# Windowed attention and a feed-forward layer in one kernel: two triangles of visible keys merged into one square, transposed once and selected apart on POOL

## The chip, the cores and the metric

One NeuronCore of a Trainium2 chip runs one program. The metric is the device time of that program in microseconds (us), the median over runs. The engines are named as in the profile: PE (TensorE), DVE (VectorE), ACT (ScalarE), POOL (GpSimd) and SP (SyncE, which here only issues transfers).

## The reference, cut to what matters

```python
# q, k, v: (B=8, H=8, S=576, D=64); w_in: (512, 2048); w_out: (2048, 512)
scores = scale * np.matmul(q, k.transpose(0, 1, 3, 2))
rel = pos[:, None] - pos[None, :]
mask = (rel >= 0) & (rel < 128)                      # each query sees itself and the 127 keys before it
scores = np.where(mask, scores + slopes[h] * -abs(rel), -1e9)
attn = exp(scores - max(scores)); attn = attn / (sum(attn) + 1e-9)
x = np.matmul(attn, v)                               # (B, H, S, D) -> 4608 tokens of 512
h = x @ w_in
out = (h / (1 + exp(-1.702 * h))) @ w_out
```

A query at position p sees the keys p-127 to p. For a block of 128 queries these lie in two blocks of 128 keys: in the block of the same positions it sees those at or below its own place (one triangle), in the block before it those above its own place (the other triangle). In columns taken modulo 128 each row therefore sees every column exactly once, and the two triangles fit together into one full square.

## The kernel before

**Feed-forward.** The 4608 tokens are taken in 18 chunks of 256. For each of 16 slices `f` of the inner width, `up(f)` makes `h_ps` with 12 products, ACT, DVE and ACT make `g` and its upper part `gh`, POOL makes its lower part `gl = g - gh`, and `down(f)` adds six products into two accumulators: `gh` by both halves of `w2` (four), then `gl` (two). Everything of 32 bits is split so into an upper and a lower part, since PE multiplies the type `fp32r`. `up(f+1)` is written ahead of `down(f)`.

**Attention** runs beside it, ahead of the chunks that need it. The first two batches (`WholeUnit`, 24 units) are multiplied in plain float32 while the weights are still being decoded. The other six batches are 24 head pairs; the change concerns these. A pair's two heads of 576 positions stand one behind the other as 1152 rows, nine blocks of 128 (`pair_blocks`); a `Unit` is two blocks, the last unit of a pair one, so a pair has five units. Block 4 holds the end of one head and the start of the next; `live` is the first column with keys of the right head (128 in block 0, which has no block before it; 64 in block 5).

A unit passes through stages, one per tick; `tick()` lets five units stand in five stages at once:

- loads of `rq`, `rk` and `rv` (SP's queue, in the order of the program), then the splits `Q`, `K1`/`K2`, `VV` on ACT, DVE and POOL
- `scores`: two products a block into `s_ps`, 128 queries by 256 keys
- `biased` (DVE): adds the mask and slope table `bias`, negates, writes `pb` and the row's minimum `mins`
- `exponents` (ACT): exponential of `pb` with its row sum; `normal` (DVE): scaling with the reciprocal `rec`
- `flip` (PE): transposes each 128x128 part of `pb` that has a key, into `t_ps`
- `high` (ACT) and `low` (DVE): the upper part `ph` and the lower part `pl` of the transposed weights
- `mix` (PE, one tick later): for each chunk of 128 keys two products into `x_ps`: all queries that see these keys (the own block and the next one, 256 columns) by the upper, then by the lower part
- `sum_up`: the sum of upper and lower rows goes to the chunk's `x`, by way of `xb` (the `carry` between two segments on POOL)

A pair has 17 of the 128x128 parts: two a block, and one in block 0.

**Order.** The program is written tick by tick: after each slice `f`, a pace worked out from the chunk that needs a batch next says whether one or more ticks follow. A scheduler then sets the order on each engine; SP's transfers, and the first eight decodings, keep the program's order. Each engine works its queue in order. Buffers rotate in pools: `rq`, `rk` three each, `pb` five, `ph` and `pl` two each.

Of the kernel before, what the change touches and what calls it, by code (L numbers as in the profile page):

```python
# [8 lines left out]
F32 = mybir.dt.float32  # L9
F32R = mybir.dt.float32r  # L10
# [10 lines left out]
P = 128  # L21
# [120 lines left out]
def tile_kernel(ctx: ExitStack, tc: tile.TileContext, q0, k0, v0, qT, kT, v, w_in, w_out, out):  # L142
# [25 lines left out]
    def tables():  # L168
# [65 lines left out]
    def load(u):  # L234
# [7 lines left out]
        u.rq = raw.tile([P, 2 * P], F32, name="rq", tag="rq")  # L242
# [4 lines left out]
    def load_whole(u):  # L247
# [5 lines left out]
        else:  # L253
            u.rq = raw.tile([P, 2 * P], F32, name="rq", tag="rq")
# [84 lines left out]
    def biased(u):  # L339
        u.mins = att.tile([P, 4], F32, name="mins", bufs=3)  # L340
        if u.whole:
            u.p = []
            for i, (at, rows) in enumerate(u.blocks):
                cs = slice(max(u.k0 - at + P, 0), P + rows)
                for hh in range(2):
                    if hh:
                        p = att.tile([P, 3 * P], F32, name="pb", tag=("K1", "K2")[i])
                    else:
                        p = att.tile([P, 2 * P], F32, name="pb", bufs=5)
# [7 lines left out]
        for e, b in enumerate(u.blocks):  # L357
            b.p = att.tile([P, 2 * P], F32, name="pb", bufs=5)
# [7 lines left out]
            if b.live > b.first:  # L366
                nc.gpsimd.memset(b.p[:, :b.live], 0.0)

    def exponents(u):
# [9 lines left out]
        for e, b in enumerate(u.blocks):  # L379
            live = b.p[:b.rows, b.live:b.end]  # L380
# [5 lines left out]
    def normal(u):  # L386
# [17 lines left out]
        for e, b in enumerate(u.blocks):  # L404
            live = b.p[:rows, b.live:b.end]
            nc.vector.tensor_scalar(live, live, u.rec[:rows, e:e + 1], None, ALU.mult)  # L406

    def flip_whole(u):
        u.pt = []
        for hh in range(2):  # L410
            t = ps.tile([P, 4 * P], F32, name="t_ps", bufs=2)
            pt = att.tile([P, 4 * P], F32, name="pw", tag=("ph", "pl")[hh])
# [16 lines left out]
    def flip(u):  # L429
# [5 lines left out]
        u.ph = att.tile([P, 4 * P], F32R, name="ph")  # L435
        u.pl = att.tile([P, 4 * P], F32R, name="pl")
        u.pspans = []
        w = 0
        for c in u.chunks:
            start = w  # L440
            for b, col in c.parts:
                nc.tensor.transpose(  # L442
                    u.t[:c.n, w:w + b.rows], b.p[:b.rows, col:col + c.n], ident[:b.rows, :b.rows])
                w += b.rows
            c.p = u.ph[:c.n, start:w], u.pl[:c.n, start:w]
            if u.pspans and u.pspans[-1][0] == c.n:
                u.pspans[-1][2] = w
            else:
                u.pspans.append([c.n, start, w])

    def high(u):
        if u.whole:
            return
        for m, a, z in u.pspans:
            nc.scalar.copy(u.ph[:m, a:z], u.t[:m, a:z])  # L455
# [318 lines left out]
```

## Time and profile before

| | |
|---|---|
| median of 3 runs | 1079.72 us (1078.15 to 1080.79) |
| profiled execution | 1078.13 us, of which 1076.2 us from first to last instruction |
| granted PE clock | 0.994 of full |
| PE busy | 1054.8 us, 98% |
| DVE, POOL, ACT busy | 706.1, 598.3, 585.7 us |

Busy time is the time in which at least one instruction of the engine runs. Products on PE overlap each other, so a product's duration is longer than the time by which it moves the next one; that time is read from rows of several products. In the groups "x408" is the number of instructions; the numbers behind the bar are the busy time, the mean duration in ns, and the idle time of the engine ahead of them with what ended it. In a stage's row the engines stand in the order PE, PEld (loading of the stationary operand), DVE, ACT, POOL, then the clock and the transfers.

### The profile page before, as it was taken

What the parts mean: (1) busy time and instruction counts of PE and PEld (TensorE: products, weight loads), DVE (VectorE), ACT (ScalarE), POOL (GpSimd) and SP (SyncE); (2) the same over time, 40 slices, a digit from 0 to 9 for tenths busy, and PEclk for the clock granted to TensorE, in tenths of its full rate; (3) what the DMA queues carried; (4) which work ended last, traced back from release to release, by engine and by line L of the source; (5) the groups of instructions that cost most, each with busy time, mean ns of one, the idle gap of its engine ahead of it and who ended that gap; (6) DMA issues with size and microseconds to landing.
All of it is one profiled execution on the core that took longest, in us unless ns stands there. A gap on an engine that the chain in (4) does not pass through costs nothing.

```text
span 1076.2 us, 21415 instructions
## 1 busy us (share of the span) xinstructions
PE 1054.8 (98%) x7041; PEld 930.7 (86%) x7041; DVE 706.1 (66%) x2195; ACT 585.7 (54%) x1773; POOL 598.3 (56%) x855
## 2 busy tenths in 40 slices
PE   8788999999999999999999999999999999999998
PEld 5566777789998999999999999999899999998987
DVE  7999953378898787645667668767868687413131
ACT  5867754366666566444555566656665556332222
POOL 3666842367676676554555657656666566323232
PEclk9989999999999999999999999999999999999999
DMA  8862101233222232111222123222222221000000
GB/s 307 294 234 59 33 13 41 67 87 88 79 81 83 63 89 66 58 27 59 65 64 66 57 64 86 65 73 66 86 66 85 56 59 46 3 18 20 1 21 19
DMA packets 88110, 78.45 MB, mean 73 GB/s; under 512 B 36800, under 2 KB 79296, under 8 KB 88000
## 3 DMA queue, kind: packets, MB, share of 16 engines
q1 hardware_dynamic: 82240, 67.14, 21.4%
q10 hardware_dynamic: 5760, 9.96, 2.5%
q8 instruction: 55, 0.90, 0.3%
q14 instruction: 55, 0.45, 0.1%
HBM read 67.63 MB, written 9.44 MB: 72 GB/s over the span
## 4 chain that ended last, share of the span: by engine, by line
PE 88%; DVE 9%; ACT 1%; issue 1%; DMA 1%; POOL 0%; SPq 0%; DVEq 0%; ACTq 0%; POOLq 0%
PE h_ps L552 35%; PE acc L571 35%; PE s_ps L334 5%; PE x_ps L499 5%; PE t_ps L442 4%; DVE wc L213 2%; DVE wc L212 2%; DVE rw L211 1%; PE x_ps L476 1%; DVE pb L351 1%; PE t_ps L419 1%; PE s_ps L324 1%; PE sb_ps L324 1%; DVE rec L392 1%; DMA rw<-w_out 1%
## 5 line engine op out<-in xcount | busy, mean ns | idle before, releaser
L562 POOL TENSOR_TENSOR gl<-g,gh 128x256 fp32r<-128x256 f32 x288 | 219.6, 763 | 295.0 <-ACT gh L561 237.2
L552 PE MATMUL h_ps<-xh,w 128*128 128x256 f32 x2304 | 373.9, 285 | 2.9 <-DVE g L558 1.8
L552 PEld LDWEIGHTS h_ps<-xh,w 128*128 128x128 f32 x2304 | 330.7, 189 | 38.2 <-DVE g L558 3.3
L571 PE MATMUL acc<-w,gh 128*128 128x512 f32 x1152 | 326.1, 400 | 1.5 <-ACT gh L561 1.4
L558 DVE SCALAR_TENSOR_TENSOR g<-g,h_ps 128x256 f32<-128x256 f32 x288 | 119.3, 415 | 192.2 <-ACT g L557 190.8
L557 ACT ACTIVATE g<-h_ps 128x256 f32<-128x256 f32 x288 | 109.7, 381 | 229.3 <-PE h_ps L552 202.1
L571 PEld LDWEIGHTS acc<-w,gh 128*128 128x128 f32 x1152 | 196.5, 189 | 30.2 <-ACT gh L561 2.4
L552 PE MATMUL h_ps<-xl,w 128*128 128x256 f32 x1152 | 194.8, 281 | 0.0
L561 ACT CAST gh<-g 128x256 fp32r<-128x256 f32 x288 | 116.6, 405 | 133.9 <-DVE g L558 125.2
L571 PE MATMUL acc<-w,gl 128*128 128x512 f32 x576 | 188.6, 402 | 0.5 <-POOL gl L562 0.5
L552 PEld LDWEIGHTS h_ps<-xl,w 128*128 128x128 f32 x1152 | 164.0, 189 | 6.0 <-POOL w L217 0.4
L312 POOL TENSOR_TENSOR K<-rk,K 128x384 fp32r<-128x384 f32 (+1 forms) x120 | 108.9, 907 | 73.8 <-ACT Q L292 15.4
L381 ACT ACTIVATE pb<-pb,mins 128x256 f32<-128x256 f32 (+2 forms) x216 | 104.9, 487 | 46.5 <-DVE mins L362 45.1
L571 PEld LDWEIGHTS acc<-w,gl 128*128 128x128 f32 x576 | 92.7, 189 | 9.1 <-POOL gl L562 0.7
L406 DVE TENSOR_SCALAR pb<-pb,rec 128x256 f32<-128x256 f32 (+2 forms) x216 | 95.2, 477 | 3.3
L311 POOL TENSOR_TENSOR Q<-rq,Q 64x256 fp32r<-64x256 f32 (+1 forms) x120 | 82.6, 688 | 19.7 <-DVE g L558 4.3
L392 DVE TENSOR_SCALAR rec<-sums 128x2 f32<-128x2 f32 (+3 forms) x144 | 49.8, 346 | 59.6 <-ACT pb L381 53.3
L362 DVE CUSTOM_DVE_ANT_0 pb<-s_ps,bias 128x256 f32<-128x256 f32 (+3 forms) x240 | 85.5, 377 | 4.9 <-PE s_ps L334 3.6
L334 PE MATMUL s_ps<-K,Q 128*128 128x256 f32 (+1 forms) x432 | 79.6, 289 | 0.5 <-DVE mins L362 0.5
L461 DVE TENSOR_TENSOR pl<-t_ps,ph 128x512 fp32r<-128x512 f32 (+2 forms) x120 | 72.1, 603 | 6.2 <-ACT ph L455 3.5
L442 PE MATMUL t_ps<-ident,pb 128*128 128x128 f32 x408 | 74.9, 272 | 0.0
L310 DVE CAST K<-rk 128x384 fp32r<-128x384 f32 (+1 forms) x120 | 50.9, 424 | 31.0 <-PE s_ps L334 29.4
(68 smaller groups left out, 1345.9 us busy)
## 6 DMA issues: line engine op xcount, KB each, us to landing
rk<-kT SPq DMA_DIRECT2D x72, 192.0 KB, 2.5
rq<-qT SPq DMA_DIRECT2D x96, 128.0 KB, 2.3
out<-o ACTq DMA_DIRECT2D x36, 256.0 KB, 2.1
rw<-w_in SPq DMA_DIRECT2D x16, 512.0 KB, 5.6
rw<-w_out SPq DMA_DIRECT2D x16, 512.0 KB, 6.5
rk<-kT SPq DMA_DIRECT2D x48, 128.0 KB, 2.2
rv<-v SPq DMA_DIRECT2D x96, 64.0 KB, 1.9
rq<-q SPq DMA_DIRECT2D x16, 128.0 KB, 2.4
```

Of the source, the lines that this page charges most:

```text
L312: nc.gpsimd.tensor_tensor(K2, rk, K1.bitcast(F32), ALU.subtract)
L334: nc.tensor.matmul(u.s[:b.rows, e, b.first:b.end], u.Q[:, b.q0 - u.q0:b.q0 - u.q0 + b.rows], k[:, ko:ko + b.end - b.first], start=(z == 0) ...
L362: nc.vector.tensor_tensor_reduce(b.p[ra:rb, cs:b.end], u.s[ra:rb, e, cs:b.end], bias[head][ra:rb, cs:b.end], -SCALE, BIG, ALU.add, ALU.min ...
L381: nc.scalar.activation(live, live, AF.Exp, bias=u.mins[:b.rows, e:e + 1], scale=-1.0, accum_out=u.sums[:b.rows, e:e + 1],)
L406: nc.vector.tensor_scalar(live, live, u.rec[:rows, e:e + 1], None, ALU.mult)
L442: nc.tensor.transpose(u.t[:c.n, w:w + b.rows], b.p[:b.rows, col:col + c.n], ident[:b.rows, :b.rows])
L552: nc.tensor.matmul(h, w1[f][:, z, k * P:(k + 1) * P], x[:, k], start=(n == 0), stop=(n == len(ops) - 1))
L557: nc.scalar.activation(g, h, AF.Tanh, scale=0.851)
L558: nc.vector.scalar_tensor_tensor(g, g, 1.0, h, ALU.add, ALU.mult)
L561: nc.scalar.copy(gh, g)
L562: nc.gpsimd.tensor_tensor(gl, g, gh.bitcast(F32), ALU.subtract)
L571: nc.tensor.matmul(acc, g[:, t * P:(t + 1) * P], w2[f][:, z], start=(f == self.f0 and n == 0), stop=(f == self.f1 - 1 and n == 2))
```

## The change

The two triangles of a block are merged before the exponential, and the merged square is transposed, split and then taken apart:

- `biased` still writes `pb` with 256 columns and takes the minimum. Columns without keys are set to a large value (`FAR`): in block 0 this is a new memset of 128x128 on POOL; in block 5 an existing memset changes its value and its place. Then DVE takes the minimum of the two halves, column by column, into the first half: in each column one of the two is masked.
- `exponents` and `normal` work on 128 columns of a block instead of up to 256.
- `flip` makes one transpose a block: 9 a pair instead of 17. `high` and `low` work on 128 columns a block, into one buffer `ph` that holds both parts.
- New in `low`: POOL selects the triangles apart. `affine_select` keeps the part on one side of the diagonal and writes zero on the other, for the upper and lower part in one instruction (128 rows by 2 x 128). One select writes the block's own half of its chunk's tile `pc`, one the second half of the chunk before: 17 a pair.
- `mix` has the same products, reading `pc`.
- To make room, `rq` has two buffers instead of three, `pb` four instead of five, `ph` one; the tiles of `flip_whole` share the four `pc` buffers, and the third unit's `rq` uses a buffer of `Q`.

```diff
+        for i, block in enumerate(blocks):
+            block.own, block.before = chunks[i], chunks[i - 1] if i else None
...
         for e, b in enumerate(u.blocks):
-            b.p = att.tile([P, 2 * P], F32, name="pb", bufs=5)
+            b.p = att.tile([P, 2 * P], F32, name="pb", bufs=4)
+            if b.live:
+                nc.gpsimd.memset(b.p[:, :b.live], FAR)
...
-            if b.live > b.first:
-                nc.gpsimd.memset(b.p[:, :b.live], 0.0)
+
+            b.p = b.p[:, :P], b.p[:, P:]
+            nc.vector.tensor_tensor(b.p[0], b.p[0], b.p[1], ALU.min)
+            b.p = b.p[0]
...
-        u.ph = att.tile([P, 4 * P], F32R, name="ph")
-        u.pl = att.tile([P, 4 * P], F32R, name="pl")
...
-            for b, col in c.parts:
-                nc.tensor.transpose(
-                    u.t[:c.n, w:w + b.rows], b.p[:b.rows, col:col + c.n], ident[:b.rows, :b.rows])
...
+        u.pt = att.tile([P, 2, 2 * P], F32R, name="ph", bufs=1)
+        for e, b in enumerate(u.blocks):
+            nc.tensor.transpose(u.t[:, e * P:(e + 1) * P], b.p, ident)
...
+        n = len(u.blocks) * P
+        nc.vector.tensor_tensor(u.pt[:, 1, :n], u.t[:, :n], u.pt[:, 0, :n].bitcast(F32), ALU.subtract)
+        for e, b in enumerate(u.blocks):
+            part = u.pt[:, :, e * P:(e + 1) * P]
+            b.own.p = att.tile([P, 2, 2 * P], F32R, name="pc", bufs=4)
+
+            nc.gpsimd.affine_select(
+                out=b.own.p[:, :, :P], in_=part, pattern=[[0, 2], [1, P]], base=0, channel_multiplier=-1,
+                compare_op=ALU.is_ge, fill=0.0)
+            if b.before:
+                nc.gpsimd.affine_select(
+                    out=b.before.p[:, :, P:], in_=part, pattern=[[0, 2], [-1, P]], base=-1, channel_multiplier=1,
+                    compare_op=ALU.is_ge, fill=0.0)
...
-                    g.x[:, a:a + c.width], c.v, c.p[z],
+                    g.x[:, a:a + c.width], c.v, c.p[:, z, :c.width],
```

The scheduler places the instructions anew. The place shown is the hand-over between two token chunks early in the blockwise attention: the last slice of one chunk (weights `w_15`) has been multiplied, and the first `gl` of the next chunk (weights `w_0`, `w_1`) is due. The names are those of the stages above; `xl` is the lower part of a chunk's `x`. On POOL, before:

```order
L538 TENSOR_TENSOR xl<-xf,xh 128x256 x2
L300 TENSOR_TENSOR VV<-rv,VV 128x2x64
L523 TENSOR_TENSOR xb<-xb,carry 64x128
L300 TENSOR_TENSOR VV<-rv,VV 128x2x64
L562 TENSOR_TENSOR gl<-g,gh 128x256
L367 MEMSET pb 128x64
L311 TENSOR_TENSOR Q<-rq,Q 64x128
L312 TENSOR_TENSOR K_4620<-rk,K_4619 128x256
L562 TENSOR_TENSOR gl<-g,gh 128x256 x2
```

On POOL now, the last twelve rows ahead of the next chunk's first two `gl`:

```order
L465 AFFINE_SELECT pc<-ph 128x2x128
L305 TENSOR_TENSOR VV<-rv,VV 128x2x64
L529 TENSOR_TENSOR xb<-xb,carry 64x128
L317 TENSOR_TENSOR K_4905<-rk,K_4904 128x384
L305 TENSOR_TENSOR VV<-rv,VV 128x2x64
L316 TENSOR_TENSOR Q<-rq,Q 64x256
L461 AFFINE_SELECT pc<-ph 128x2x128
L465 AFFINE_SELECT pc<-ph 128x2x128
L461 AFFINE_SELECT pc<-ph 128x2x128
L465 AFFINE_SELECT pc<-ph 128x2x128
L365 MEMSET pb 128x128
L568 TENSOR_TENSOR gl<-g,gh 128x256 x2
```

Before, three POOL instructions of attention stood between two `gl` here; now 35 stand between the `gl` of `w_15` and that of `w_0`, 17 of them selects (the first 24 are not shown).

On PE, before, from the products of attention at that place to the first that reads the new chunk's `gl`:

```order
L499 MATMUL x_ps<-ph,VV 128x256
L499 MATMUL x_ps<-pl,VV 128x256
L442 MATMUL t_ps<-ident,pb 128x128 x4
L552 MATMUL h_ps<-xh,w_2_578 128x256 x8
L552 MATMUL h_ps<-xl,w_2_578 128x256 x4
L499 MATMUL x_ps<-ph,VV 128x256
L552 MATMUL h_ps<-xh,w_3_598 128x256 x4
L571 MATMUL acc_4589<-w_0_457,gh 128x512 x2
L571 MATMUL acc_4589<-w_0_457,gl 128x512
```

On PE now:

```order
L558 MATMUL h_ps<-xh,w_3_598 128x256 x7
L577 MATMUL acc_4690<-w_0_457,gh 128x512
L577 MATMUL acc_4691<-w_0_457,gh 128x512
L577 MATMUL acc_4690<-w_0_457,gh 128x512
L577 MATMUL acc_4691<-w_0_457,gh 128x512
L505 MATMUL x_ps<-pc,VV 128x256 x2
L558 MATMUL h_ps<-xh,w_3_598 128x256
L558 MATMUL h_ps<-xl,w_3_598 128x256 x4
L339 MATMUL s_ps<-K_4904,Q 128x256
L577 MATMUL acc_4690<-w_0_457,gl 128x512
L577 MATMUL acc_4691<-w_0_457,gl 128x512
```

The products that read `gl` have moved behind other work: ahead of the first of them now stand all of `up(3)` and a product of scores. From the last product by the `gl` of `w_15` to the first by the `gl` of `w_0`, PE has 42 products of `h_ps`, 18 of `x_ps`, 11 of `s_ps`, 8 transposes and 4 of the accumulators.

More of the change, by code (lines that the diff above doesn't have):

```diff
@@ L171, in tables @@
         make_identity(nc, ident)
-        rel_i = raw.tile([P, 2 * P], I32, name="rel_i", tag="rq")
+        rel_i = raw.tile([P, 2 * P], I32, name="rel_i", tag="rq", bufs=2)
         nc.gpsimd.iota(rel_i, pattern=[[-1, 2 * P]], base=P, channel_multiplier=1)
-        rel = raw.tile([P, 2 * P], F32, name="rel", tag="rq")
+        rel = raw.tile([P, 2 * P], F32, name="rel", tag="rq", bufs=2)
         nc.vector.tensor_scalar(rel, rel_i, -1.0 / SCALE, None, ALU.mult)
@@ L241, in load @@
         u.nk = u.q0 + u.nq - u.k0
-        u.rq = raw.tile([P, 2 * P], F32, name="rq", tag="rq")
+        u.rq = raw.tile([P, 2 * P], F32, name="rq", tag="rq", bufs=2)
         u.rk = raw.tile([P, 3 * P], F32, name="rk", tag="rk")
@@ L253, in load_whole @@
         else:
-            u.rq = raw.tile([P, 2 * P], F32, name="rq", tag="rq")
+            if u.at == DEPTH - 1:
+                u.rq = att.tile([P, 2 * P], F32, name="rq", tag="Q")
+            else:
+                u.rq = raw.tile([P, 2 * P], F32, name="rq", tag="rq", bufs=2)
             u.rk = raw.tile([P, 3 * P], F32, name="rk", tag="rk")
@@ L348, in biased @@
                     else:
-                        p = att.tile([P, 2 * P], F32, name="pb", bufs=5)
+                        p = att.tile([P, 2 * P], F32, name="pb", bufs=4)
                     e = 2 * i + hh
@@ L379, in exponents @@
         for e, b in enumerate(u.blocks):
-            live = b.p[:b.rows, b.live:b.end]
+            live = b.p
             nc.scalar.activation(
@@ L404, in normal @@
         for e, b in enumerate(u.blocks):
-            live = b.p[:rows, b.live:b.end]
-            nc.vector.tensor_scalar(live, live, u.rec[:rows, e:e + 1], None, ALU.mult)
+            nc.vector.tensor_scalar(b.p, b.p, u.rec[:rows, e:e + 1], None, ALU.mult)
     def flip_whole(u):
@@ L411, in flip_whole @@
             t = ps.tile([P, 4 * P], F32, name="t_ps", bufs=2)
[L412 removed]
+            pt = att.tile([P, 4 * P], F32, name="pw", tag="pc", bufs=4)
             u.pt.append([])
@@ L434, in flip @@
         u.t = ps.tile([P, 4 * P], F32, name="t_ps", bufs=2)
-        u.ph = att.tile([P, 4 * P], F32R, name="ph")
-        u.pl = att.tile([P, 4 * P], F32R, name="pl")
[L437 to L440, printed above, removed]
-            for b, col in c.parts:
-                nc.tensor.transpose(
-                    u.t[:c.n, w:w + b.rows], b.p[:b.rows, col:col + c.n], ident[:b.rows, :b.rows])
[L444 to L449, printed above, removed]
+        u.pt = att.tile([P, 2, 2 * P], F32R, name="ph", bufs=1)
+        for e, b in enumerate(u.blocks):
+            nc.tensor.transpose(u.t[:, e * P:(e + 1) * P], b.p, ident)
     def high(u):
[L452 to L455, printed above, removed]
+        if not u.whole:
+            n = len(u.blocks) * P
+            nc.scalar.copy(u.pt[:, 0, :n], u.t[:, :n])
     def low(u):
@@ L459, in low @@
             return
-        for m, a, z in u.pspans:
-            nc.vector.tensor_tensor(u.pl[:m, a:z], u.t[:m, a:z], u.ph[:m, a:z].bitcast(F32), ALU.subtract)
+        n = len(u.blocks) * P
+        nc.vector.tensor_tensor(u.pt[:, 1, :n], u.t[:, :n], u.pt[:, 0, :n].bitcast(F32), ALU.subtract)
[9 more added lines that the diff above has]
+                    compare_op=ALU.is_ge, fill=0.0)
     open_x = {}
```

## The prediction

> **What bounds the kernel now.** I read the page's busy times and slices first, then the busy times by stage, then PE's waits.
>
> ```profile
> span 1076.2 us, 21415 instructions
> PE 1054.8 (98%) x7041; PEld 930.7 (86%) x7041; DVE 706.1 (66%) x2195; ACT 585.7 (54%) x1773; POOL 598.3 (56%) x855
> ...
> PE   8788999999999999999999999999999999999998
> ...
> DVE  7999953378898787645667668767868687413131
> ...
> POOL 3666842367676676554555657656666566323232
> PEclk9989999999999999999999999999999999999999
> ```
>
> PE is busy throughout at full clock; DVE and POOL are well below, but not evenly. The stages below are cut between head pairs of the blockwise attention, whose first scores stand at 215.6 us (first row): five pairs to 342.6, three to 422.7, six to 642.3, then the rest. Columns are busy us, with instructions in brackets.
>
> ```profile
> L334 PE MATMUL s_ps<-K,Q x432: 218/280/388, 215.6 to 913.4; 128*128 128x256 f32 x120, 128*128 128x128 f32 x24
> ...
> 0.00:225.90 225.90, 209.36 (x1295) 155.75 (x1296) 161.20 (x432) 137.77 (x421) 121.51 (x127) 0.98 0.39 128
> 225.90:342.60 116.70, 116.24 (x815) 106.73 (x814) 102.48 (x333) 77.22 (x240) 82.28 (x128) 1.00 0.30 85
> 342.60:422.70 80.10, 80.10 (x558) 73.97 (x557) 59.67 (x207) 49.30 (x153) 52.18 (x82) 1.00 0.27 73
> 422.70:642.30 219.60, 219.60 (x1497) 201.84 (x1495) 137.70 (x449) 113.39 (x346) 122.86 (x187) 1.00 0.21 59
> 642.30:930.00 287.70, 287.62 (x1982) 264.96 (x1981) 209.90 (x700) 168.82 (x518) 176.92 (x277) 1.00 0.23 65
> 930.00:1076.20 146.20, 141.83 (x905) 127.48 (x903) 35.12 (x78) 39.23 (x100) 42.58 (x57) 0.99 0.04 15
> ...
> 642.30:695.70 53.40, 53.40 (x372) 49.33 (x371) 41.38 (x140) 33.25 (x105) 35.39 (x56) 1.00 0.27 74
> ...
> 732.20:810.50 78.30, 78.22 (x539) 71.73 (x538) 59.00 (x198) 47.44 (x149) 49.98 (x78) 1.00 0.26 72
> ```
>
> Columns: PE, weight loads, DVE, ACT, POOL. From 225.9 on PE is the bound; in the first five pairs DVE is at 102.5 and POOL at 82.3 of 116.7. A busy PE could still be a loosely packed one, so I take the spacing of products that stand in a row, and what PE waited for.
>
> ```profile
> L552 PE MATMUL h_ps<-xh,w 128*128 128x256 f32 x2304 | 373.9, 285 | 2.9 <-DVE g L558 1.8 <-DVE xh L536 0.9 <-ACT w L216 0.2
> L571 PE MATMUL acc<-w,gh 128*128 128x512 f32 x1152 | 326.1, 400 | 1.5 <-ACT gh L561 1.4
> L442 PE MATMUL t_ps<-ident,pb 128*128 128x128 f32 x408 | 74.9, 272 | 0.0
> ...
> 445.15 1.10 PE L552 MATMUL h_ps<-xh,w 128*128 128x256 f32 x8
> 444.44 0.63 PE L571 MATMUL acc<-w,gh 128*128 128x512 f32 x2
> 441.79 0.71 PE L442 MATMUL t_ps<-ident,pb 128*128 128x128 f32 x5
> ...
> 441.29 0.73 POOL L562 TENSOR_TENSOR gl<-g,gh 128x256 fp32r<-128x256 f32 x1 [2.25 <-ACT gh L561]
> 443.98 0.19 PEld L571 LDWEIGHTS acc<-w,gl 128*128 128x128 f32 x1
> ...
> PE acc L571 <- POOL gl L562: 0.5, 1, 0.5
> ```
>
> Spacing: h (1.10-0.285)/7 = 0.116 us, acc 0.63-0.40 = 0.23, transpose (0.71-0.272)/4 = 0.11. PE's only wait on POOL's gl in the whole run was 0.5 us; in the row shown, gl ended at 442.02 and was used at 443.98, 2.0 us of slack.
>
> **The change, part by part.**
>
> *PE.* A head pair had 17 transposes and has 9 (the order shows them, so that the merge might not take place is no rival): 24 x 8 = 192 fewer, at 0.11 us: -21.1 us, 4.4 of it in the first five pairs. Scores and value products stay. I take the spacing and not the mean of a transpose, 272 ns: that much of each overlaps its neighbours. The Trainium skill (TensorE: Matmul & The Clock Gate, Part 4) gives about 275 ns for a transpose inside a kernel; the row agrees as a duration, and by it the saving would be 53 us, more than the spacing allows.
>
> *POOL.* New are 17 selects a pair (408) and one memset of 128x128 a pair.
>
> ```profile
> L177 POOL TENSOR_SCALAR_AFFINE_SELECT rel<-rel 128x256 f32<-128x256 f32 x2 | 0.8, 398 | 0.3 <-DVE rel L175 0.2
> masks.py:197 POOL MEMSET ident<- 128x128 f32 x1 | 0.2, 204 | 0.3 <-POOLq L770 0.3
> L402 POOL TENSOR_SCALAR pb<-pb,rec 128x256 f32<-128x256 f32 x12 | 13.5, 1133 | 10.6 <-DVE rec L393 5.8 <-ACT wc L210 2.6 <-PE h_ps L552 2.1
> L562 POOL TENSOR_TENSOR gl<-g,gh 128x256 fp32r<-128x256 f32 x288 | 219.6, 763 | 295.0 <-ACT gh L561 237.2 <-issue 17.6 <-PE acc L571 8.7
> L312 POOL TENSOR_TENSOR K<-rk,K 128x384 fp32r<-128x384 f32 x72 | 73.4, 1019 | 45.8 <-PE x_ps L499 11.0 <-ACT Q L292 8.1 <-DVE K L310 7.3
> L311 POOL TENSOR_TENSOR Q<-rq,Q 64x256 fp32r<-64x256 f32 x96 | 71.2, 742 | 15.5 <-DVE g L558 3.5 <-DVE K L310 1.6 <-DVE xf L529 1.5
> L300 POOL TENSOR_TENSOR VV<-rv,VV 128x128 fp32r<-128x128 f32 x96 | 46.5, 484 | 9.8 <-ACT VV L299 6.2 <-DVE K L310 1.7 <-POOL Q L311 0.5
> L523 POOL TENSOR_TENSOR xb<-xb,carry 64x128 f32<-64x128 f32 x48 | 22.4, 466 | 7.0 <-ACT xb L520 6.1
> ```
>
> The same operation on as many elements took 398 ns, but alone, at the start. The far upper end is the nearest other one-input operation of that size, 1133 ns: 462 us more, POOL saturated everywhere, near 1290. I take 0.42, since it is the same operation, and keep up to 0.6 in the range for work beside a busy DVE. A pair then costs POOL 17 x 0.42 + 0.2 = 7.3 us.
> First five pairs: 82.3 + 36.7 = 119.0 on POOL against 116.7 - 4.4 = 112.3 on PE. POOL becomes the bound there. The order says where: from one gl to the next, at the hand-over to a new token chunk, stand 17 selects, 4 K, 4 Q, 5 VV, 2 xb, 3 memsets and the gl: with each kind at its largest row 7.1 + 4.1 + 3.0 + 2.4 + 0.9 + 0.6 + 0.8 = 18.9 us, while PE between the matching products has 71 of 0.116, 8 transposes and 6 acc, 10.5 us. So 8 us too much, less what of the 2.0 of slack is left: some 7 us of wait for gl there; queued behind it on PE are those acc products and all that follows. With its neighbours I take +9.
> Later pairs: three to 422.7 need 52.2 + 22.0 = 74.2 of 80.1 - 2.6 = 77.5; two to 695.7, 35.4 + 14.7 = 50.1 of 51.6; three to 810.5, 50.0 + 22.0 = 72.0 of 75.7. It fits at 95 to 97%, the 2.0 us of slack being the cover; I take +3 for the places where it doesn't.
>
> *DVE.*
>
> ```profile
> L538 DVE TENSOR_TENSOR xl<-xf,xh x34: 406/902/979, 94.9 to 1025.5; 128x256 fp32r<-128x256 f32 x34
> L538 POOL TENSOR_TENSOR xl<-xf,xh x34: 740/786/1049, 91.7 to 1024.2; 128x256 fp32r<-128x256 f32 x34
> L526 DVE TENSOR_TENSOR carry<-x_ps,xb 64x128 f32<-64x128 f32 x48 | 13.3, 277 | 8.2 <-ACT xb L520 5.2 <-POOL xb L523 2.8
> L406 DVE TENSOR_SCALAR pb<-pb,rec x216: 279/354/1629, 220.4 to 916.4; 128x256 f32<-128x256 f32 x84, 128x128 f32<-128x128 f32 x12, 128x192 f32<-128x192 f32 x12
> L461 DVE TENSOR_TENSOR pl<-t_ps,ph 128x512 fp32r<-128x512 f32 x72 | 48.9, 683 | 3.9 <-PE x_ps L499 2.0 <-ACT ph L455 1.3
> L461 DVE TENSOR_TENSOR pl<-t_ps,ph 128x256 fp32r<-128x256 f32 x24 | 10.0, 416 | 1.4 <-ACT ph L455 1.2
> ```
>
> New are 9 minima a pair, two SBUF inputs, 128 columns: 0.277 each by the carry's row, 2.5 us a pair. Low parts shrink from 683 to 416, four times, -1.1. The scaling halves its columns but its 279 ns minimum says little is won: -0.5 at best. Net +0.9 a pair with POOL quiet. With POOL running, DVE's own two-SBUF-input row goes from 406 to a median of 902, while POOL's goes only from 740 to 786: DVE is the one that waits. Doubling the minima and the slowed scaling bounds it at +4.8 a pair. In the first five, 102.5 + 4.5 to 24 = 107 to 126.5; I take the middle, 117, under POOL's 119, and +3 for two full engines that wait on each other. Later pairs stay under PE: 59.7 + 14.4 = 74.1 of 77.5 at worst.
>
> *ACT* loses half the columns of the exponentials and high parts; off the path (54%), worth nothing.
>
> *Fewer buffers.* Two rq instead of three, pb four instead of five, one ph.
>
> ```profile
> 13.98 0.38 SPq L154 DMA_DIRECT2D rq<-q  x1
> 20.61 0.33 SPq L154 DMA_DIRECT2D rq<-q  x1
> ```
>
> The load at 13.98 will wait for the scores that released the one at 20.61, 6.6 us later, and SP's queue (K loads, two weights) with it. Between nothing and 6.6; loads are issued ticks ahead of their use, so I take +1.
>
> **Sum.** -21.1 + 9 + 3 + 3 + 1 = -5.1. The profiled execution took 1078.1 (its span and 1.9 us around it), 1.6 below the median of the three: 1073 against it, 1074.6 against the median. Forecast 1075. Its own range is 1066 to 1076.4, 0.3% (3.2 us) being about the least that a measurement of this kernel tells from no change.
>
> **Rivals.**
> - *Everything is hidden.* For it: PE waited 0.5 us for gl in all. Against: 119.0 on POOL against 112.3. All of -21.1, 1059.
> - *A wash.* DVE reaches its upper end in the first five pairs (126.5 instead of 112.3, +14.2) and takes +3 later: -21.1 + 14.2 + 3 + 1, about 1077; anything to 1083.
> - *The select is dearer under load; slower.* At 0.5 the first five pairs need 82.3 + 43.5 = 125.8 of POOL, +9 over before, and the rest's 16.7 is about spent on the 95% groups: that is the point from which it decides. At 0.6: 134.3, +17.6 over 116.7; the three groups above 83.4, 56.2 and 81.2, together +9 over before; the sparse rest -6: about 1100. For it: L402's 1133. Against: gl's 763 and xl's 786 hardly move under load.
> - *DVE's minima and scalings exclude POOL's work and add to it.* 9 x (0.277 + 0.279) = 5.0 a pair on top of POOL: 119 + 25 = 144 in the first five, +27; the three groups 89, 60 and 87, +24; sparse pairs -5: about 1126. For it, DVE's 902; against, POOL's 786. The Trainium skill (SBUF — State Buffer, Who interferes with whom) states it as a rule: whichever of the two starts first holds the shared port pair for its whole instruction and the other blocks fully. The trace agrees for DVE; for POOL it shows 46 ns.
>
> **How the numbers follow.** Forecast 0.34, all hidden 0.11, wash 0.19, dearer select 0.24, exclusion 0.08, the far end or a late load 0.04. Faster by over 0.3% is the first two, 0.45; same 0.19; slower 0.36. The range 1060 to 1102 leaves out half of the all-hidden case, the upper part of the dearer select, and the exclusion: about 2 in 10.
>
> **What would show it.** Right: 216 transposes at the same spacing; selects at 0.40 to 0.45; waits of acc products for gl of 5 to 12 us, nearly all between 225 and 345, none above 1 us after; minima of 0.3 to 0.5. Wrong: selects above 0.5; PE waiting for gl or for x products past 345; waits for DVE's g in place of POOL's gl; a later first blockwise score than 215.6 us.

## The result, and the profile after

Slower: 1106.96 us (median of 4 runs, 1104.64 to 1108.33) against 1078.94 for the kernel before beside it (4 runs), a ratio of 1.0262 (95% interval 1.0247 to 1.0277). The forecast was 1075 with a range of 1060 to 1102.

The page of the changed kernel: busy times, tenths of the span, chain of waits by engine.

```profile
span 1106.6 us, 21847 instructions
PE 1054.4 (95%) x6849; PEld 917.8 (83%) x6849; DVE 766.7 (69%) x2411; ACT 553.1 (50%) x1773; POOL 763.7 (69%) x1287
...
PE   8879999999987999999999999999999999999998
...
DVE  6899943378897798764687869786889778423131
...
POOL 3666843378898888865787878987888888523232
PEclk9988999999998999999999999999999999999999
...
PE 65%; DVE 24%; issue 4%; ACT 3%; POOL 3%; DMA 1%; SPq 0%; DVEq 0%; POOLq 0%; ACTq 0%
```

PE has 192 products fewer (6849 for 7041) and a hole near slice 12, just past 300 us. Its busy time has not fallen all the same, 1054.4 us for 1054.8, and its idle time has risen from 21.4 to 52.2. The saving is not lost by this: transposes in a row still start 0.109 us apart at the median in both kernels. But a product shown as 0.28 us moves the next by only 0.12, so a short wait between two products stands in PE's busy time: products of `h_ps` by `xh` in a row start 118 and then 117 ns apart at the median, but 121 and then 127 in the mean (read from 200 us on). DVE holds 24% of the chain that ended last; POOL holds 3% although it got the selects. By stages (columns as in the prediction: PE, weight loads, DVE, ACT, POOL, then PE's granted clock), the kernel after and then the kernel before:

```profile
233.40:366.60 133.20, 118.58 (x764) 105.32 (x764) 112.18 (x383) 69.59 (x243) 116.00 (x218) 0.96 0.28 76
...
300.00:350.00 50.00, 38.32 (x235) 32.84 (x236) 44.39 (x151) 25.30 (x89) 44.23 (x85) 0.93 0.32 84
350.00:950.00 600.00, 585.06 (x3903) 529.63 (x3902) 460.94 (x1541) 308.85 (x1027) 486.91 (x894) 1.00 0.23 63
```

```profile
300.00:350.00 50.00, 49.54 (x342) 45.34 (x341) 42.84 (x141) 31.93 (x100) 34.34 (x53) 1.00 0.29 81
350.00:950.00 600.00, 599.92 (x4109) 552.02 (x4109) 408.94 (x1349) 332.20 (x1013) 353.08 (x545) 1.00 0.22 62
```

The first row is the first five head pairs, cut at the same marks as the prediction's 116.7 us (a memset of `pb` that comes once a pair): they took 133.2 us, and yet no engine is full there (PE 118.6, DVE 112.2, POOL 116.0). What PE waited for, in total us, times, longest:

```profile
PE x_ps L505 <- DVE xf L535: 8.0, 11, 1.9
PE h_ps L558 <- DVE g L564: 7.1, 11, 1.0
PE h_ps L558 <- DVE xh L542: 4.9, 11, 0.8
PE t_ps L445 <- DVE ph L456: 3.5, 3, 1.5
PE h_ps L558 <- ACT w L218: 3.0, 1, 3.0
PE t_ps L445 <- DVE pb L414: 2.8, 3, 1.3
```

All but one are for DVE, and that one, for a decoded weight, lies in the first 200 us. The acc products waited 0.7 us for POOL's `gl`, the score products 1.3 for its selects. The groups of the new and the touched operations (busy us, mean ns, idle time ahead):

```profile
L375 DVE TENSOR_TENSOR pb<-pb 128x128 f32<-128x128 f32 x216 | 102.3, 499 | 0.7 <-POOL pb L368 0.2
L414 DVE TENSOR_SCALAR pb<-pb,rec 128x128 f32<-128x128 f32 x216 | 94.4, 473 | 2.8
L461 POOL TENSOR_SCALAR_AFFINE_SELECT pc<-ph 128x256 fp32r<-128x256 f32 x216 | 93.2, 432 | 17.4 <-DVE ph L456 12.4
L465 POOL TENSOR_SCALAR_AFFINE_SELECT pc<-ph 128x256 fp32r<-128x256 f32 x192 | 80.1, 424 | 0.0
```

and single lines with the minimum, median and maximum of their durations in ns, first of the changed kernel, then one of the kernel before:

```profile
L375 DVE TENSOR_TENSOR pb<-pb x216: 271/485/2091, 223.6 to 944.8; 128x128 f32<-128x128 f32 x108
L461 POOL TENSOR_SCALAR_AFFINE_SELECT pc<-ph x216: 398/409/668, 234.4 to 953.6; 128x256 fp32r<-128x256 f32 x108
L542 DVE CAST xh<-xf x68: 274/490/1366, 90.2 to 1054.5; 128x256 fp32r<-128x256 f32 x68
```

```profile
L536 DVE CAST xh<-xf x68: 278/290/831, 91.3 to 1024.1; 128x256 fp32r<-128x256 f32 x68
```

The selects on POOL stay near their minimum of 398. The minima on DVE have 485 in the middle, but not evenly: the 35 that start while POOL runs nothing (memsets aside) take 275 to 295, the 181 others 489 at the median. The cast `xh` (`L536` before, `L542` after), which the change doesn't touch, went from 290 to 490 at the median; its mean went from 459 to 529, since many were held before too. The timeline shows how (start, us, operation):

```profile
339.53 0.45 POOL L305 TENSOR_TENSOR VV<-rv,VV 128x128 fp32r<-128x128 f32 x1
339.65 1.20 DVE L315 CAST K<-rk 128x256 fp32r<-128x256 f32 x1
339.69 0.69 PE L445 MATMUL t_ps<-ident,pb 128*128 128x128 f32 x2 [1.49 <-DVE ph L456]
...
339.94 0.41 POOL L461 TENSOR_SCALAR_AFFINE_SELECT pc<-ph 128x256 fp32r<-128x256 f32 x1
...
340.30 0.41 POOL L465 TENSOR_SCALAR_AFFINE_SELECT pc<-ph 128x256 fp32r<-128x256 f32 x1
```

A cast that takes 0.29 with POOL idle lasted 1.20 us, through three of POOL's operations that follow each other without a gap (to 340.71), and ended soon after them. POOL's own took their usual time.

POOL is held as well, but for less. Of the 408 selects, 188 start while DVE runs one of the operations that read SBUF alone (minima, scalings, `xl`, the casts `K` and `xh`): 108 of these take over 450 ns, at most 668. Of the 220 others two do, at most 468. Where DVE still has 200 to 300 ns to go when a select starts, the select takes 115 ns more than its 408 at the median. In sum the selects lose some 8 us (their mean is 428), the minima some 47 (499 for the 279 that is the median of the 35).

To see where along the run time is lost, I read from the traces when the 33rd, the 65th and the last of the 288 `gl` began. The 65th is the first of the fifth token chunk, which holds the first rows of the blockwise attention; in every run here the products of that batch's four head pairs end 4 to 20 us ahead of it. I call the stretch from the 33rd to the 65th the **hand-over**. The columns are the three stretches in us. Behind the 65th some twenty pairs are left, whose share of PE's saving is about 17 us.

| kernel | to the 33rd | to the 65th (hand-over) | to the last |
|---|---|---|---|
| before | 198.5 | 128.7 | 742.0 |
| after | 198.5 | 151.5 | 749.6 |

The hand-over takes 22.8 us more. Behind it, where some 17 should be won, 7.6 are lost: another 25.

### The profile page after: what moved, and what is told of

It is laid out like the page before. It is cut to its first block, busy times and chain, and to the rows that moved or that the text cites. A ratio compares the mean times of both kernels' runs of the same rounds, so it can differ in the third digit from the quotient of the medians.

```text
span 1106.6 us, 21847 instructions
## 1 busy us (share of the span) xinstructions
PE 1054.4 (95%) x6849; PEld 917.8 (83%) x6849; DVE 766.7 (69%) x2411; ACT 553.1 (50%) x1773; POOL 763.7 (69%) x1287
## 4 chain that ended last, share of the span: by engine, by line
PE 65%; DVE 24%; issue 4%; ACT 3%; POOL 3%; DMA 1%; SPq 0%; DVEq 0%; POOLq 0%; ACTq 0%
PE h_ps L558 27%; PE acc L577 26%; PE x_ps L505 3%; PE s_ps L339 3%; DVE pb L375 3%; DVE pb L414 2%; DVE pb L369 2%; DVE wc L215 2%; DVE wc L214 2%; DVE K L315 2%; DVE xh L542 2%; DVE g L564 2%; DVE xf L535 2%; PE x_ps L482 1%; ACT pb L390 1%
## 5 line engine op out<-in xcount | busy, mean ns | idle before, releaser
L564 DVE SCALAR_TENSOR_TENSOR g<-g,h_ps 128x256 f32<-128x256 f32 x288 | 119.0, 414 | 175.5 <-ACT g L563 174.8
L577 PEld LDWEIGHTS acc<-w,gh 128*128 128x128 f32 x1152 | 198.3, 189 | 32.9 <-ACT gh L567 3.0
L558 PE MATMUL h_ps<-xl,w 128*128 128x256 f32 x1152 | 199.3, 282 | 0.0
L567 ACT CAST gh<-g 128x256 fp32r<-128x256 f32 x288 | 116.7, 406 | 144.1 <-DVE g L564 137.1
L577 PE MATMUL acc<-w,gl 128*128 128x512 f32 x576 | 186.2, 401 | 0.7 <-POOL gl L568 0.7
L558 PEld LDWEIGHTS h_ps<-xl,w 128*128 128x128 f32 x1152 | 168.2, 190 | 8.4 <-issue 0.7
L390 ACT ACTIVATE pb<-pb,mins 128x128 f32<-128x128 f32 x216 | 86.3, 400 | 113.0 <-DVE pb L375 107.9
L461 POOL TENSOR_SCALAR_AFFINE_SELECT pc<-ph 128x256 fp32r<-128x256 f32 x216 | 93.2, 432 | 17.4 <-DVE ph L456 12.4
L375 DVE TENSOR_TENSOR pb<-pb 128x128 f32<-128x128 f32 x216 | 102.3, 499 | 0.7 <-POOL pb L368 0.2
L316 POOL TENSOR_TENSOR Q<-rq,Q 64x256 fp32r<-64x256 f32 (+1 forms) x120 | 86.0, 716 | 17.8 <-ACT Q L297 2.9
L414 DVE TENSOR_SCALAR pb<-pb,rec 128x128 f32<-128x128 f32 x216 | 94.4, 473 | 2.8
L505 PE MATMUL x_ps<-pc,VV 128*128 128x256 f32 (+1 forms) x432 | 78.7, 286 | 8.7 <-DVE xf L535 8.0
L465 POOL TENSOR_SCALAR_AFFINE_SELECT pc<-ph 128x256 fp32r<-128x256 f32 x192 | 80.1, 424 | 0.0
```

Source lines behind the costliest of these rows:

```text
L375: nc.vector.tensor_tensor(b.p[0], b.p[0], b.p[1], ALU.min)
L414: nc.vector.tensor_scalar(b.p, b.p, u.rec[:rows, e:e + 1], None, ALU.mult)
L505: nc.tensor.matmul(g.x[:, a:a + c.width], c.v, c.p[:, z, :c.width], start=(c is g.first and z == 0), stop=(c is g.last and z == 1), skip_g ...
L558: nc.tensor.matmul(h, w1[f][:, z, k * P:(k + 1) * P], x[:, k], start=(n == 0), stop=(n == len(ops) - 1))
L564: nc.vector.scalar_tensor_tensor(g, g, 1.0, h, ALU.add, ALU.mult)
L567: nc.scalar.copy(gh, g)
```

## The experiments

**The theory P with which they began:** the saving on PE is real, and the work put on DVE and POOL eats it, largely because DVE's operations with both operands in SBUF stand still while POOL works. **Rivals:** POOL's time alone (with the port innocent), the fewer buffers, or a PE list that is not what bounds. Times are medians; each ratio is to the kernel before on the same chip.

### Taking away one part each

```diff
 # e1: the selects (both), POOL -> ACT, same shapes, nothing selected
-            nc.gpsimd.affine_select(out=b.own.p[:, :, :P], in_=part, ...)
+            nc.scalar.copy(b.own.p[:, :, :P], part.bitcast(F32))
 # e2: no minima
-            nc.vector.tensor_tensor(b.p[0], b.p[0], b.p[1], ALU.min)
-            b.p = b.p[0]
+            b.p = b.p[1]
 # e3: the kernel BEFORE with the changed kernel's two raw q and four score tiles
 # e4: the scalings on ACT
-            nc.vector.tensor_scalar(b.p, b.p, u.rec[:rows, e:e + 1], None, ALU.mult)
+            nc.scalar.activation(b.p, b.p, AF.Copy, scale=u.rec[:rows, e:e + 1])
```

> The changed kernel with its 408 selects replaced by copies of the same shape on ACT (the triangles are not taken apart, so the masking is left out). POOL goes back to about 600 us busy, ACT rises by about 165 us; DVE's work is unchanged. Theory P (DVE's instructions that read or write two ways through SBUF wait for POOL's, DVE becomes late, PE waits for it): the minimum falls from a mean of 499 ns to about 420, the scaling from 473 to about 400, time 1065 to 1085. Rival Q (POOL's queue is simply too full): the time falls as far, 1060 to 1070, but with the minimum still near 500. Rival C (the chain of a unit has become longer, whatever engine does it): no better, 1100 to 1110.

> The changed kernel without the 216 minima: only the half with the block's own keys goes on (the other triangle is left out of the result). DVE has about 102 us less, POOL keeps all selects. Theory P: PE's waits for DVE go, 1065 to 1080. Rival Q: POOL is as full as before, at most 5 us better, 1100 to 1107. Rival C: half a microsecond less in each unit's chain, 1090 to 1100.

> The kernel before with only the smaller buffer counts of the change: two rq, pb four, the third unit's rq in a buffer of Q. If the buffers carry the loss: 1085 to 1100. Theories P, Q and C: 1078 to 1081, and the first blockwise scores within 2 us of 215.6.

> The changed kernel with the 216 scalings of the blockwise part on ACT instead of DVE. DVE has about 94 us less, ACT about 85 us more (640 us, 58%), POOL the same. Theory P: 1068 to 1085, and the minimum no longer than 499 ns. Rival Q: 1100 to 1107. Rival C: 1103 to 1110, since a unit's chain keeps all its steps.

Measured: e1 1080.88 us (1.0024, 1.0013 to 1.0034), e2 1085.94 (1.0073, 1.0052 to 1.0094), e3 1087.5 (1.0092, 1.0070 to 1.0114), e4 1096.43 (1.0167, 1.0149 to 1.0186). Against 1107, moving the selects off POOL wins 26, leaving out the minima 21, moving the scalings off DVE 10.5; the two counts of buffers cost the kernel before 8.9. e2 and e4 fell between the ranges of P and of its rivals: each part costs, and none is the whole. Two of the groups of e1:

```profile
L375 DVE TENSOR_TENSOR pb<-pb 128x128 f32<-128x128 f32 x216 | 102.0, 500 | 0.6
L414 DVE TENSOR_SCALAR pb<-pb,rec 128x128 f32<-128x128 f32 x216 | 80.7, 411 | 2.2
```

The minima are as long without the selects: POOL's other work is enough to hold them (I had expected 420). So the selects' 26 us do not come through the minima; what is left is POOL's own time in a block's chain and DVE's other operations, of which the scalings gain 62 ns each; how the 26 divide between these two is not shown. That POOL's time is the whole cause is excluded by e2 and e4, which leave the selects where they are.

### The port by itself, and the buffers in the changed kernel

```diff
 # e9: the minimum's first input straight from the raw scores in PSUM (not the biased ones)
-            nc.vector.tensor_tensor(b.p[0], b.p[0], b.p[1], ALU.min)
+            nc.vector.tensor_tensor(b.p[0], u.s[:, e, P:], b.p[1], ALU.min)
 # e5: control; to make room, the last two slices of w_out use the one before them
 # e6: e5 with rq 3, pb 5, ph 2, pc 6        # e7: e5 with rq 3, pb 5
```

> The changed kernel with the first input of the minimum taken from the scores in PSUM instead of the biased half in SBUF: the same 216 instructions of the same size, one SBUF input instead of two (the first half's bias is left out of the result). Theory P (two SBUF inputs make DVE wait for POOL): the minimum falls from a mean of 499 ns to 280 to 320, 45 us of DVE's time, and the kernel to 1090 to 1100. If the minimum's 499 ns have another cause: still 450 or more, 1104 to 1110.

> Control for the next two: the changed kernel with the last two slices of w_out left out (slice 13's tile is used in their place), so that 8 KB a partition are free and unused. Two of 32 decodings fewer, each some 3 us of DVE while DVE is full: 1099 to 1107 under every theory.

> The control with the freed room used: three rq, five pb, two ph, six pc (the last two slices of w_out left out as in the control). Theory B (the change's scarce buffers couple the engines: new selects wait for products of the unit before, the next upper part waits for selects): 15 us or more below the control. Theory L (the load on DVE and POOL itself, stretched where both use SBUF, is the loss): 5 to 9 us below it, what the counts cost the kernel before (8.9 us), and PE's waits for DVE stay.

> The control with only the old counts restored, three rq and five pb; one ph, four pc (the last two slices of w_out left out). Theory L: 5 to 9 us below the control and equal to the run with all buffers within 3 us. Theory B: at least half of the gain of all buffers is missing here.

Measured: e9 1090.21 (1.0117, 1.0098 to 1.0136); e5 1110.88 (1.0299, 1.0284 to 1.0315), e6 1101.1 (1.0207, 1.0192 to 1.0223), e7 1106.37 (1.0255, 1.0236 to 1.0274). The minima of e9:

```profile
L375 DVE TENSOR_TENSOR pb<-s_ps,pb x216: 260/291/293, 223.2 to 931.6; 128x128 f32<-128x128 f32 x108
```

The same count, width and place, one input from PSUM: the median falls from 485 to 291 and the maximum from 2091 to 293, and the kernel is 16.8 us faster. With the 35 quiet minima of the changed kernel (275 to 295) that settles the port: what slows the minimum is its second input from SBUF while POOL works. The Trainium skill (SBUF — State Buffer, Who interferes with whom) says that a DVE instruction with at most one SBUF input, outside the two-port modes, does not contend with GpSimd; e9 agrees. The same section of the Trainium skill has the order of issue decide who blocks. Both sides show it here, the 181 minima that start beside POOL's work and the 188 selects that start beside DVE's; but where POOL's operations follow each other, DVE waits for the whole row of them, and so DVE loses more. Buffers: against their control e5, all of them back are worth 9.8 us, the two old counts 4.5. So the scarce `ph` and `pc` count as well, some 5 us, though not the 15 that would make buffers the main cause. The control itself is 3.9 above the changed kernel and above the range I gave for it; why is not known.

### What is left when the work is gone, and a merge without two SBUF inputs

e10 has neither minima nor selects (and without `pc` its `ph` tiles rotate in five buffers). e11 is complete: the merge is a predicated copy within PSUM, ahead of the biasing, which then is 128 wide; the four `pb` tiles hold a unit's two squares each. e12 adds the scalings on ACT, e13 leaves out the addition of 1e-9 to the sums.

```diff
 # e11 (the table `bias` is folded to 128 columns once; rows of other heads are set to -FAR first)
+            before, own = u.s[:, e, :P], u.s[:, e, P:]
+            nc.vector.copy_predicated(own, masks[0], before)
-                    b.p[ra:rb, cs:b.end], u.s[ra:rb, e, cs:b.end], bias[head][ra:rb, cs:b.end],
+                    b.p[ra:rb], own[ra:rb], bias[head][ra:rb, :P],
                     -SCALE, BIG, ALU.add, ALU.min, u.mins[ra:rb, e:e + 1],
-            nc.vector.tensor_tensor(b.p[0], b.p[0], b.p[1], ALU.min)
```

> The changed kernel without its 216 minima and without its 408 selects: each block's square is its own half of the scores, and the products with v read the transposed square as it stands, in the same number and shape, so the output is not the reference's. PE's list is that of the changed kernel (216 transposes). Theory P (the saving on PE is real, and what ate it is the work on DVE and POOL, the port and the buffers): 1078.5 - 21 for 192 transposes, + 4 to + 9 for the two raw q and four score tiles that stay fewer = 1062 to 1068. Rival R (the transposes that went were not on the path, PE is held by something that the change does not touch): 1073 to 1080, with the spacing of PE's products longer than before in the later pairs too.

> The changed kernel, complete, with another merge: DVE copies the keys of the block before into the places of the own half's later keys while both are raw scores in PSUM (one predicated copy of 128x128 per block, its mask in SBUF), then biases and takes the row minimum of 128 columns in place of 256; no operation of the merge has two inputs in SBUF. One 128x256 tile holds a unit's two squares, so the four tiles are twice as many squares. Theory P (DVE's time decides): minima 499 ns gone, 216 copies of 0.28 us from the row of the 128-wide operations that read PSUM, 128-wide biasing instead of 256-wide (279 for 415 ns), 72 short memsets: DVE's busy time some 700 to 720 us, close to the run without minima (692) and below the one with the first input from PSUM (733), so 1082 to 1088, some 4 us of it through the buffers. Rival Q (a copy from PSUM to PSUM costs as much as the minimum did, 0.45 us or more): 1098 to 1106.

> The same kernel with the 216 scalings on ACT, which alone won 10.5 us in the changed kernel. Theory P (DVE is what PE waits for): DVE near 620 to 640 us, ACT near 615; 1072 to 1079. Rival (with the port freed the scalings are hidden on DVE already, or ACT in the chain of gh holds PE): no more than 3 us below the kernel with the scalings on DVE.

> The same kernel without the addition of 1e-9 to the sums ahead of the reciprocal (a sum is at least 1, where it changes nothing in 32 bits): 120 short DVE operations less, 96 of them 331 ns long in the changed kernel though they hold two columns. Theory P (DVE's time and the chain of a block's softmax count): 3 to 7 us below the kernel with it, 1067 to 1075. Rival (off the path by then): within 2 us of it.

Measured: e10 1068.4 (0.9910, 0.9896 to 0.9925), e11 1095.9 (1.0168, 1.0153 to 1.0184), e12 1086.2 (1.0081, 1.0066 to 1.0096), e13 1081.28 (1.0033, 1.0019 to 1.0047).

e10 lies 0.4 above P's range, and R falls: PE's saving is there when its neighbours have less to do. Its stretch behind the hand-over is 727.0 us, 15 less than before, of the 17 forecast. e11, e12 and e13 each came out 6 to 8 us above what I expected, though the steps between them (-9.7, -4.9) are as foretold and the copy has the price of its row:

```profile
L380 DVE COPY_PREDICATED s_ps<-later,s_ps x216: 273/295/297, 223.4 to 944.3; 128x128 f32<-128x128 uint8 x108
```

So something else was left. The same table:

| kernel | to the 33rd | hand-over | to the last |
|---|---|---|---|
| e1 selects as copies on ACT | 197.3 | 140.9 | 733.9 |
| e2 no minima | 195.9 | 146.2 | 733.1 |
| e9 one input from PSUM | 198.3 | 152.0 | 730.3 |
| e10 neither minima nor selects | 197.9 | 135.0 | 727.0 |
| e13 merge in PSUM, ACT scales, no addition | 193.9 | 150.6 | 728.0 |

Behind the hand-over, e9 and e13 have 11.7 and 14.0 of the 17 us that were forecast; their whole loss is the hand-over, 22 to 23 us, as large as in the changed kernel, although DVE has less to do there in e13 than in the kernel before (33.05 for 42.84 us):

```profile
300.00:350.00 50.00, 40.38 (x230) 34.65 (x229) 33.05 (x137) 33.05 (x114) 43.82 (x83) 0.83 0.31 89
350.00:950.00 600.00, 599.13 (x4040) 548.83 (x4039) 350.79 (x1364) 369.97 (x1209) 475.04 (x851) 1.00 0.23 65
```

From 300 to 350 PE works 40.4 of 50 us, and its granted clock is 0.83 where it is 1.00 later; DVE and ACT work 33, POOL 43.8. PE's rows of e13 in that place:

```profile
317.83 0.33 PE L453 MATMUL t_ps<-ident,pb 128*128 128x128 f32 x1
320.47 0.77 PE L513 MATMUL x_ps<-pc,VV 128*128 128x256 f32 x2 [2.31 <-DVE xf L543]
...
325.56 0.33 PE L453 MATMUL t_ps<-ident,pb 128*128 128x128 f32 x1 [1.46 <-ACT pb L422]
...
336.71 1.51 PE L513 MATMUL x_ps<-pc,VV 128*128 128x256 f32 x6 [1.95 <-POOL VV L305]
```

PE waits in turn for DVE, ACT and POOL. From 315.9 to 338.2 us its list has only products of attention; the longest such stretch of more than 20 products is 10.5 us in the changed kernel, and the kernel before has none. In the list of e13, from the first score of each of the first four pairs to that of the next, stand 8.2, 8.9, 8.1 and 1.0 slices of the feed-forward (counted by products of `h_ps`); before, 6.0, 6.0, 6.4 and 5.6. So the slices that could have covered a block's chain seem to have been spent early; e14 tries it.

### The hand-over, the buffers again, and controls

```diff
 # e14: e13 with the blocks due eight slices earlier   # e17: the same line alone, in the changed kernel
-SLACK = 2
+SLACK = 10
 # e15: the kernel BEFORE with the scalings on ACT, no addition, SLACK 10
 # e16: e14 with rq 3, ph 2, pc 6 (w_out as in e5)     # e8: the kernel BEFORE with two raw q, five score tiles
 # e18: e14, complete, with rq 3 in the place of one score tile
```

> The complete kernel with the merge in PSUM, the scalings on ACT and no addition (1081.3 us), with SLACK 10 in place of 2: the blocks of a batch are put due eight steps earlier. In PE's list of that kernel the first four blockwise pairs have 8.2, 8.9, 8.1 and then 1.0 of the feed-forward's steps between them, and in its trace 18.8 us of PE's idle time lie between 300 and 350 us, in a stretch of 22 us with products of attention alone; with the constant at 10 the list has 7.6, 8.5, 7.2 and 5.3. Theory P (what is left of the loss is the stretch without feed-forward's products ahead of the fifth slice, where PE waits through a block's chain): 7 to 13 us less, 1068 to 1074, below the kernel before. Rival R (the pairs end when DVE, ACT and POOL are through with them, however the steps are spread): 1079 to 1083, the idle time spread over the first three pairs.

> Control: the kernel before with the three edits that have nothing to do with the merge: scalings on ACT, no addition to the sums, SLACK 10. Theory P (from 250 us on PE idles 4.5 us in all in the kernel before, so DVE's time is not what it waits for): 1075 to 1080. Rival (these edits alone are a gain, and the merge has no part in it): 1068 to 1074.

> The kernel with the merge in PSUM, scalings on ACT, no addition and SLACK 10, with three raw q, two squares ph and six pc, for which the last two slices of w_out are replaced by the one before (a wrong output; the control of the changed kernel with that replacement was 3.9 us slower than the changed kernel). Theory P (buffers still cost 5 to 10 us): 5 to 9 us below the same kernel with fewer, 1060 to 1067. Rival: within 2 us of it, since ACT and DVE now give buffers free early.

> The kernel before with two raw q in place of three, and the whole unit's q in the place of Q, as the change has it, but five score tiles. With four score tiles as well it was 8.9 us slower than before. If the raw q cost it: 1083 to 1088. If the fifth score tile does: 1078 to 1081. I take the first, since the q are loaded by the one queue in order and the start of the first eight slices was late already (16th slice at 143.8 against 135.4 us).

> Control: the changed kernel with nothing else than SLACK 10. Theory P (its minima, scalings and selects load DVE and POOL in every pair, and only a kernel with DVE relieved can use the earlier start): 1098 to 1106, DVE's share in the first pairs above 80 per cent as before. Rival O (the place of the steps in PE's list is the main loss): 1085 to 1095.

> The complete kernel with the merge in PSUM, scalings on ACT, no addition and SLACK 10 (1075.2 us), with three raw q again; their place comes from the score tiles (three instead of four, a unit's two squares in one; a whole unit's third tile uses the place of ph). Theory P (the third raw q is worth what it was): all buffers together gave 3.3 us there, so 1070 to 1074. Rival (PE's list has 4.1 steps in the fourth pair in place of 5.3, and one place for the whole units' third tile makes them wait): 1075 to 1080.

| kernel | us | ratio (95%) | to the 33rd | hand-over | to the last |
|---|---|---|---|---|---|
| e14 | 1075.21 | 0.9965 (0.9952 to 0.9978) | 196.2 | 139.6 | 729.3 |
| e15 before, other edits | 1078.65 | 1.0000 (0.9991 to 1.0010) | 203.0 | 126.3 | 742.0 |
| e16 | 1071.89 | 0.9933 (0.9918 to 0.9947) | 200.8 | 132.6 | 730.1 |
| e8 before, two raw q | 1088.95 | 1.0091 (1.0074 to 1.0108) | 204.8 | 133.8 | 743.4 |
| e17 after, SLACK 10 | 1117.8 | 1.0369 (1.0341 to 1.0396) | 203.1 | 149.8 | 758.3 |
| e18 | 1073.28 | 0.9959 (0.9940 to 0.9977) | 199.0 | 138.7 | 729.6 |

- **e14**: the hand-over falls by 11 us of the 22, the time by 6.1, just under what I expected (7 to 13). (For e13 I had put 18.8 us of idle time between 300 and 350 us; its row above has 50 - 40.4 = 9.6.) The complete kernel is now faster than the kernel before, by 0.35%. The windows of e14 and e18 show that the hole is smaller, not closed, with POOL still the fullest beside PE:

```profile
300.00:350.00 50.00, 43.61 (x269) 38.50 (x269) 33.37 (x137) 32.91 (x110) 43.19 (x81) 0.90 0.29 82
```

```profile
300.00:350.00 50.00, 44.05 (x264) 38.17 (x264) 33.11 (x137) 34.00 (x116) 43.80 (x82) 0.90 0.28 80
```

- **e15**: the other edits alone are worth nothing in the kernel before. The gain of e14 and e18 is the merge's, once DVE and the list let it through.
- **e17**: the order of the list alone does not help the changed kernel; it is 11 us slower than without, beyond both expectations. The loss lies ahead of the 33rd `gl` (4.6 us) and behind the hand-over (8.7). Its PE waits longer for DVE's `g`, where the changed kernel had 7.1 us in 11 waits; why the earlier start does this is not shown:

```profile
PE h_ps L558 <- DVE g L564: 13.8, 17, 2.0
```

- **e8**: the third raw q alone carries what e3 showed (1088.95 against 1087.5), the score tile nothing that shows. SP's waits, first in e8, then in the kernel before:

```profile
SPq L154 <- PE sb_ps L327: 150.0, 17, 17.2
```

```profile
SPq L154 <- PE sb_ps L324: 96.2, 17, 11.8
```

The 17 loads that wait for scores of the whole batches wait 3.2 us longer each, 54 us on SP's queue. The time grows by some 6 us ahead of the 33rd `gl` and 5 in the hand-over. That this comes from these loads is read, not shown: other waits on the queue change too (for POOL's `Q` from 115.9 to 438.1 us, for its `VV` from 342.1 to 71.1).

- **e16 and e18**: with the buffers, 3.3 and 1.9 us less than e14. e16 is above its range of 1060 to 1067, and it leaves out two slices of w_out, which alone cost the changed kernel 3.9. e18 is the fastest of the complete kernels, 0.41% below the kernel before. Its interval overlaps that of e14, so that the third raw q helps there is not shown.

## Why the prediction was wrong

The sum was -21.1 (PE) + 9 (POOL in the first pairs) + 3 (later pairs) + 3 (DVE) + 1 (buffers). Divided by the stretches, it had some 8 us more in the hand-over, where 22.8 were measured, and some 15 less behind it, where 7.6 more were measured. So the larger part of the error lies in the later pairs. Point by point:

- **PE, -21.1: right in kind, nearly so in size.** Behind the hand-over some 17 were to come; e10 has 15.0, e13 14.0, e9 11.7.
- **The selects' price: right.** 0.42 forecast, 424 and 432 ns measured. **Their consequence: wrong.** I had PE wait for `gl`, some 7 us at the hand-over; it waited 0.7. The order did show 17 selects between two `gl` there, but PE was held up ahead of them, mostly by DVE.
- **The step that failed first: the fullest engine sets the stage's time.** For the first five pairs I had POOL 119.0, DVE 117, PE 112.3, and by the sum 112.3 + 9 + 3 = 124.3 us. The measured busy times are 116.0, 112.2, 118.6; the stage took 133.2. Three engines at 84 to 89% that pass a block from one to the next wait for each other, and the sum had "+3 for two full engines that wait on each other" for this. PE's own 118.6 is over the 112.3 as well, at a granted clock of 0.96 for 1.00; the sum had no term for that. e10 took the work from both and had all but 6 of the hand-over's 23 us back; e13 took it from DVE alone, with a more uneven list, and had 1.
- **The later pairs, +3, and "stay under PE": wrong by most.** 7.6 lost where about 17 were to be won. The step compared each engine's work with PE's time, found 95 to 97% for POOL and at worst 74.1 of 77.5 for DVE, and so charged almost nothing. DVE's 460.9 us of 600 is indeed not full, but it was late at the places where PE needs `g`, `xh` and `xf`. e9 alone gives 19 of the 25 back, and e1, which leaves the minima at 500 ns, 16: relieving either engine is nearly enough, so it is the two loads together that were too much there.
- **DVE, +3, nothing later: its busy time was foreseen, its price was not.** The first five pairs have 112.2 for 117. But leaving the minima out won 21, moving the scalings 10.5. In the reading of the rows: the minimum was taken at the carry's 277 ns, bounded at twice that, and is 499, 60 of the 216 above the bound. The scaling's minimum of 279 ns belongs to 128 columns; 256 took 334 at least, so halving does win time, but beside POOL the 128 columns took 473 in the mean. And "DVE is the one that waits" is half of it: POOL's selects wait too, for less.
- **Buffers, +1: too small.** In the kernel before, two raw q for three cost 10.3 us (e8); in the changed kernel the two old counts are worth 4.5 and all buffers 9.8 (e7, e6). The prediction had the place and the rows, the load that waits 6.6 us for other scores, and set it aside because loads are issued ticks ahead.

Of the rivals, exclusion (1126) had the mechanism in part right: DVE's operations and POOL's hold each other up. But they do so only where they meet, and POOL loses little, so the works don't add to a sum. The rival nearest in time, the dearer select (about 1100), is near by luck: the selects were not dearer. Of the signs of being right, the transposes, the selects and the minima came, the waits for `gl` did not. Of the signs of being wrong came waits for DVE's `g` in place of `gl`, waits for x products past 345 us, and a later first blockwise score (220.5 us).

Shown by runs: the port (e9), what the selects, minima and scalings are worth (e1, e2, e4), the cost of the raw q (e8), that PE's saving exists (e10), that the list's order is part of the rest in e13 (e14, with e15 as the control; in the changed kernel the same line loses, e17). Only read from traces: that the remaining 10 us in the hand-over of e18 are POOL's time in a block's chain; no run here took the selects off POOL in that kernel. How the hand-over's 22.8 us divide between DVE, POOL and the lower clock stays open. The gains of the single parts don't add: e1 and e2 alone win 26 and 21, both together 38.5, with more buffers for the squares.

## What to carry to other kernels

Three engines at some 85% that pass blocks to one another can lengthen a stage though none is full: ask for the chain of one block through all of them and for the deadline that ends it, not for the largest busy sum. Before an elementwise operation is added on DVE beside a busy POOL, look where its inputs lie: here, with one of them in PSUM the minimum kept its quiet time, with both in SBUF it waited, and so did the casts and scalings already there, before the change too. Where a buffer is given up, look in the transfer queue for the load that will wait for it; that it is issued early did not cover it here.

## What the runs showed of the hardware that was not expected

- DVE lost much, POOL little: the 128x128 minimum took 271 to 2091 ns, the select 398 to 668 with a median of 409. Which of the two waits went by who ran first: minima that started without POOL 275 to 295, beside it 489 at the median; selects that started beside such DVE work 454 at the median, the others 408. A DVE cast of 0.29 us lasted 1.20 through three POOL operations in a row.
- Half the columns won nothing beside a busier POOL: the scaling of 128x128 took 473 ns in the mean in the changed kernel, that of 128x256 in the kernel before 458. Started while POOL ran nothing, they took 281 and 347 at the median.
- A predicated copy from PSUM to PSUM, 128x128 with its mask in SBUF, took 273 to 297 ns beside POOL at 67% busy (e11), as e9's minimum with one input in PSUM did (260 to 293).
- Where PE's list had a hole, its granted clock fell as well: 0.93 from 300 to 350 us in the changed kernel, 0.83 in e13, 0.90 in e14, against 1.00 in the kernel before, and 1.00 from 350 to 950 us in the changed kernel and in e13.
